# A cached-attention block on one core: start of TensorE's work, order of K's transposes, and where its instruction pages begin

## The chip, the core and the metric

The kernel runs on one core of a Trainium2 chip. A core has engines with queues of their own that meet through semaphores: TensorE (matmuls, shown as PE, its weight loads as PEld), VectorE (DVE), ScalarE (ACT), GpSimd (POOL) and SyncE (SP), which here issues the DMAs. The metric is the device time of the whole kernel in microseconds (us), the median of several runs.

## The reference

```
B, Sq, D = 8, 112, 640;  H, Sk, Dh = 32, 512, 192        # all inputs bf16
q = (x @ wq).reshape(B, Sq, H, Dh).transpose(0, 2, 1, 3)
scores = einsum("bhqd,bhkd->bhqk", q, k_cache) * Dh ** -0.5
o = einsum("bhqk,bhkd->bhqd", softmax(scores), v_cache)
return o.transpose(0, 2, 1, 3).reshape(B, Sq, H * Dh) @ wo
```

A query projection for 896 rows, attention of 112 queries over 512 cached keys for each of 8 x 32 batch and head pairs, and an output projection. K and V are read once each; together they are most of the 117.5 MB that the profile counts as read.

## The kernel before, in words

`build_main` treats the heads in NG = 8 groups of four. A **unit** is one group with one batch entry, so there are NU = 64 units; unit u has g = u // 8 and b = u % 8. All loops are unrolled and every engine's order is written out by hand. (A second, slower kernel stands behind a flag for inputs out of range; it doesn't run here.)

**TensorE per unit i:** `do_S(i)`, scores of unit i, 96 matmuls of 32 rows, four of them abreast; `do_T(i - 2)`, six transposes of the normalised outputs; a slot (i, 0); `do_PV(i - 1)`, 16 matmuls; a slot (i, 1). A slot holds a **pair** or half of one (`do_pair`): a chunk of the query projection of the next group ("Q", 5 steps), or a 128-row tile of the output projection ("O", 6 steps). A step is one weight load and a matmul for each half of the row, into PSUM banks 6 and 7; the second matmul (`held`) uses the weights that are loaded. Before a pair's first step `bank_free` waits until the pair before has been copied out: a Q by ScalarE, an O by VectorE (`do_OE`). FILL cuts the matmuls of chosen slots, all but the first step's, into several narrower ones; this adds instructions and no arithmetic.

**VectorE per unit i:** transposes of K tiles (`do_KT(u, t)`, four a unit, from the landed `kr` to `kt`), the first three of the unit's list; `do_OE` of slot 0; `do_NM(i - 1)`, sums, reciprocals and half of the normalisation; `do_OE` of slot 1; the rest of its transposes. `kt_ahead` says how many tiles are done at the end of unit i: 4(i + 2) and a few more. `kr` has three buffers; SyncE issues K's load of unit u once the transposes of unit u - 3 are done, V's once PV of unit u - 4 is.

**The start:** TensorE keeps itself busy with WARM + 1 matmuls on the identity, transposes four of the seven 128-row tiles of x (`do_X`, one PSUM bank each), which VectorE (m = 0, 2) and ScalarE (m = 1, 3) copy to xT. Then come six chunks of the first group's projection for the first half of the rows (`do_Q0(c, 0)`); their weights are taken from the landed wq by a stride, in four column strips of 32. In the meantime GpSimd reorders the same weights into `wq0` (`reorder`, semaphore gW0). Then the last three tiles of x, S(0), and six chunks for the other half of the rows with `wq0`.

Kernel lines that the text names: L843 x transposes, L847 `held`, L863 and L870 first projections, L905 pairs, L924 S, L945 PV, L956 T, L962 warm-up, L1082 K transposes, L1103 and L1106 copies of O, L1111 copies of x by VectorE, L1180 reorder.

## Time and profile before

| | us |
|---|---|
| median of 12 runs | 401.61 |
| lowest, highest | 399.4, 406.86 |
| the profiled execution, device time | 400.95 |
| its span, first to last instruction | 398.9 |
| TensorE busy | 387.6 |
| VectorE, ScalarE, GpSimd busy | 293.0, 254.2, 140.7 |

"Busy" is the time in which an engine had an instruction in work; TensorE's matmuls overlap, so it is told not from that share but from the distance of their starts whether TensorE goes at its pace. The row of DMA shows 8 to 9 tenths in nearly all of the span, at 350 to 377 GB/s up to 80 us and about 310 after that. "issue" as a releaser means that an engine waited for nothing that the profile shows.

### The profile page before, as it was taken

The page shows a single profiled execution, that of the slowest core. Times are in us where ns is not written, and L with a number is a line of the kernel's source. Part 1 is how long each engine was busy: PE and PEld are TensorE (multiplying, and loading weights), DVE is VectorE, ACT ScalarE, POOL GpSimd, SP SyncE. Part 2 cuts the span into 40 slices and gives each one's busy share as a digit, 9 for nine tenths or more (in the row PEclk, how much of TensorE's full clock was granted, in tenths as well). Part 3 has the DMA queues.
Part 4 walks back from the last instruction along what each step waited for, and adds up shares of the span by engine and source line. Part 5 has one row for each costly group of instructions (what it writes and reads, how often), then busy time and mean ns, then how long its engine had stood idle before and what let it go on. Part 6 is the DMA issues. An engine that isn't in the chain of part 4 may idle for free.

```text
span 398.9 us, 20213 instructions
## 1 busy us (share of the span) xinstructions
PE 387.6 (97%) x9073; PEld 243.1 (61%) x8291; DVE 293.0 (73%) x569; ACT 254.2 (64%) x550; POOL 140.7 (35%) x420
## 2 busy tenths in 40 slices
PE   7999999999999999999999999999999999999995
PEld 3556564656656555565665666656565665667672
DVE  1667768787796686876787776886788677799833
ACT  3667764766656765558756676566774766666662
POOL 6513543243333253333451254232344223223320
PEclk9999999999999999999999999999999999999999
DMA  8999999999998999989999999989999889999711
GB/s 275 377 372 351 350 353 363 356 314 317 348 329 272 318 325 291 302 287 298 339 317 307 302 305 321 335 274 313 296 306 318 263 276 341 314 293 286 228 37 67
DMA packets 88443, 120.04 MB, mean 301 GB/s; under 512 B 9760, under 2 KB 88352, under 8 KB 88352
## 3 DMA queue, kind: packets, MB, share of 16 engines
q1 hardware_dynamic: 88352, 118.72, 90.0%
q8 instruction: 69, 1.13, 1.2%
q14 instruction: 22, 0.18, 0.2%
HBM read 117.54 MB, written 1.15 MB: 298 GB/s over the span
## 4 chain that ended last, share of the span: by engine, by line
PE 86%; SPq 5%; DMA 3%; DVE 3%; issue 2%; DVEq 0%
PE ps L847 20%; PE ps L945 20%; PE ps L924 19%; PE ps L905 18%; PE ps L956 6%; SPq L1290 5%; DMA kr<-in_k_cache_dram 3%; DVE kt L1082 2%; PE ps L870 2%; PE ps L863 1%; DMA xs<-in_x_dram 1%; PE ps L843 1%; DVE xs L1106 0%; DVE acc L1103 0%; DVE acc L1106 0%
## 5 line engine op out<-in xcount | busy, mean ns | idle before, releaser
L1082 DVE STREAM_TRANSPOSE kt<-kr 128x384 int32<-128x384 int32 x256 | 191.9, 867 | 11.2 <-DMA kr<-in_k_cache_dram 10.8
L1023 ACT ACTIVATE pT<-ps 128x448 bf16<-128x448 f32 x256 | 130.7, 562 | 75.9 <-PE ps L924 75.9
L945 PE MATMUL ps<-vs,pT 128*128 128x193 bf16 x512 | 95.2, 247 | 1.1 <-issue 1.0
L924 PEld LDWEIGHTS ps<-qT,kt 32*128 32x128 bf16 x6144 | 77.1, 93 | 30.4 <-issue 24.4
L905 PE MATMUL ps<-wos,oT 128*128 128x320 bf16 x342 | 90.7, 289 | 2.2 <-DVE acc L1103 1.5
L847 PE MATMUL ps<-wos,oT 128*128 128x320 bf16 (+3 forms) x470 | 92.1, 267 | 0.2
L1206 POOL TENSOR_SCALAR bad<-rinv 112x4 f32<-112x4 f32 x64 | 14.6, 228 | 214.7 <-DVE rinv L1091 214.7
L924 PE MATMUL ps<-qT,kt 32*128 32x112 bf16 x6144 | 87.7, 208 | 1.1 <-issue 1.0
L945 PE MATMUL ps<-vm,pT 128*128 128x193 bf16 x512 | 85.0, 247 | 0.5 <-issue 0.5
L847 PE MATMUL ps<-xT,wqs 128*128 128x448 bf16 (+4 forms) x282 | 74.5, 309 | 0.0
L905 PE MATMUL ps<-xT,wqs 128*128 128x448 bf16 (+2 forms) x210 | 72.8, 347 | 0.2 <-DVE acc L1106 0.2
L1030 ACT ACTIVATE os<-ps,rinv 112x192 bf16<-112x192 f32 x128 | 46.8, 417 | 38.5 <-DVE rinv L1091 37.3
L1188 POOL COPY vm<-vs 128x384 int32<-128x384 int32 x128 | 61.2, 508 | 17.0 <-issue 8.7
L905 PEld LDWEIGHTS ps<-wos,oT 128*128 128x128 bf16 x342 | 33.2, 97 | 47.3 <-issue 39.4
L1007 ACT ACTIVATE qT<-ps 128x448 bf16<-128x448 f32 x96 | 48.1, 554 | 17.0 <-PE ps L905 10.8
L945 PEld LDWEIGHTS ps<-vs,pT 128*128 128x128 bf16 x512 | 47.7, 97 | 18.0 <-ACT oT L1040 10.6
L1088 DVE TENSOR_REDUCE sm<-ps 112x4 f32<-112x8 f32 x64 | 10.6, 165 | 53.9 <-PE ps L945 53.9
L1106 DVE TENSOR_TENSOR acc<-ps,acc 128x320 f32<-128x320 f32 x84 | 37.2, 485 | 16.5 <-PE ps L905 16.5
L945 PEld LDWEIGHTS ps<-vm,pT 128*128 128x128 bf16 x512 | 46.6, 97 | 4.5 <-issue 1.8
L1040 ACT ACTIVATE oT<-ps 128x672 bf16<-128x672 bf16 x64 | 46.4, 725 | 1.9 <-PE ps L956 1.9
L905 PEld LDWEIGHTS ps<-xT,wqs 128*128 128x128 bf16 x210 | 20.4, 97 | 35.0 <-issue 30.2
L1094 DVE TENSOR_TENSOR os<-ps,rinv 112x384 bf16<-112x384 f32 x64 | 35.7, 558 | 6.5
(42 smaller groups left out, 174.5 us busy)
## 6 DMA issues: line engine op xcount, KB each, us to landing
kr<-in_k_cache_dram SPq DMA_DIRECT2D x256, 192.0 KB, 4.0
vs<-in_v_cache_dram SPq DMA_DIRECT2D x256, 192.0 KB, 3.9
wos<-in_wo_dram SPq DMA_DIRECT2D x48, 160.0 KB, 4.0
wqr<-in_wq_dram SPq DMA_DIRECT2D x35, 192.0 KB, 5.2
out_dram<-xs SPq DMA_DIRECT2D x7, 160.0 KB, 2.1
wqs<-in_wq_dram SPq DMA_DIRECT2D x5, 192.0 KB, 3.8
xs<-in_x_dram SPq DMA_DIRECT2D x2, 320.0 KB, 3.3
xs<-in_x_dram SPq DMA_DIRECT2D x1, 480.0 KB, 5.4
```

The costliest lines, as they stand in the source:

```text
L847: return pe.add_instruction(mybir.InstMatmult(name=nc.get_next_instruction_name(), engine=mybir.EngineType.PE, ins=[pe.lower_ap_or_imm(rhs ...
L905: mm = (pe.matmul if h == hs[0] and f == 0 else held)(ps[:, 6 + h, cs], w, rhs[h][:, cs], q == 0, q == n - 1 and f == cuts - 1)
L924: mm = pe.matmul(ps[:, a, SQ * t:SQ * (t + 1)], kt[u % NT][p, t, c // 2, :, c % 2], qT[g % 2][p, c, SQ * b:SQ * (b + 1)], start=(c == 0), ...
L945: mm = pe.matmul(pv[:, k, e, o0:o0 + DH + 1], pT[u % 2][:, a, t, :], src[:, a, v0:v0 + DH + 1], start=(t == 0), stop=(t == 3), skip_group_ ...
L1007: act.activation(qT[g % 2][:, c, HQ * h:HQ * (h + 1)], ps[:, 6 + (n % 2 if g == 0 else h), 0:HQ], ACTF.Copy).then_inc(aQ, 1)
L1023: act.activation(pT[u % 2][:, a, :, 0:SQ], ps[:, a, 0:4 * SQ].rearrange("p (t q) -> p t q", t=4), ACTF.Exp, scale=scale).then_inc(aEX, 1)
L1030: ins = act.activation(os_[u % 2][:, DH * (2 + e):DH * (3 + e)], pv_of(u)[0:SQ, 1, e, 1:1 + DH], ACTF.Copy, scale=rinv[:, u % 4, 2 + e:3 + e])
L1040: act.activation(oT[:, :, SQ * b:SQ * (b + 1)].rearrange("p (k c) q -> p k c q", k=2), src.rearrange("p k (c q) -> p k c q", c=3), ACTF.Co ...
L1082: dve.transpose(dst, src).then_inc(vKT, 1)
L1094: dve.tensor_tensor(os_[u % 2][:, 0:2 * DH].rearrange("p (e d) -> p e d", e=2), pv[0:SQ, 0, :, 1:1 + DH], rinv[:, u % 4, 0:2][:, :, None]. ...
L1106: ins = dve.tensor_tensor(ob[:, m, cs] if g == NG - 1 else acc[:, m, cs], src, acc[:, m, cs], op=ALU.add)
L1188: ins = gp.tensor_copy(vm[u % NM][:, :, (DH + 2) * h:(DH + 2) * h + DH].bitcast(I32), vs[u % NV][:, :, 32 + DH * (1 + h):32 + DH * (2 + h) ...
```

## The change

- Warm-up: matmuls of 4 x WN = 120 columns instead of 80. The tuple that brings WN also sets WARM to 20; the older line `WARM = 30` stays below it.
- After the first four tiles of x, BRIDGE = 8 matmuls of 128 columns on the identity.
- Tile m = 3 of x is transposed into two banks (3 and 5); ScalarE copies its first two chunks, VectorE the other three, as third of its copies. The counts that others wait for (vX) go up by one.
- Chunks c >= RAW = 4 of the first half use `wq0`, with 5 matmuls of full width instead of 20 of 32 columns, and wait for gW0.
- FILL: the cuts at units 24, 48 and in the last group go; slots (32, 0) and (32, 1) are cut in 2 and 3.
- `kt_ahead`: one tile ahead up to unit 9, then one more every second unit, five from unit 16 (before: one more every fifth unit, five from unit 20).

TensorE's main program goes from 9073 matmuls and 8291 weight loads to 8865 and 8262. The queues of SyncE and GpSimd keep their instructions and order.

```diff
-    FILL = {(24, 0): 5, (24, 1): 6, (48, 0): 4, (48, 1): 5, **{(i, j): 2 for i in range(56, 64) for j in range(2)}}
+    FILL = {(32, 0): 2, (32, 1): 3}
+    WARM, WN, BRIDGE, RAW = 20, 30, 8, 4
     HINT_AT = {"act": 55, "dve": 60, "pool": 53, "sp": 56}
     WARM = 30
...
-        want = min(4 * (i + 2) + min(5, 1 + i // 5), 4 * NU)
+        want = min(4 * (i + 2) + min(5, 1 + max(0, i - 8) // 2), 4 * NU)
...
-                    mm = pe.transpose(psb[:, m, dc * 128:(dc + 1) * 128], xs[:, m, dc * 128:(dc + 1) * 128], ident[:])
+                    mm = pe.transpose(psb[:, 5 if m == 3 and dc >= 2 else m, dc * 128:(dc + 1) * 128], xs[:, m, dc * 128:(dc + 1) * 128], ident[:])
...
-                    W(pe, vX, 2 if h == 0 else 3)
+                    W(pe, vX, 3 if h == 0 else 4)
...
-                    if h == 1:
-                        if c == 0:
+                    if h == 1 or c >= RAW:
+                        if h == 0 and c == RAW:
                             W(pe, gW0, dc + 1)
-                        mm = pe.matmul(ps[:, 6 + n % 2, 0:HQ], wq0[:, dc, 128 * c:128 * (c + 1)], xT[:, dc, HQ:2 * HQ],
+                        mm = pe.matmul(ps[:, 6 + n % 2, 0:HQ], wq0[:, dc, 128 * c:128 * (c + 1)], xT[:, dc, HQ * h:HQ * (h + 1)],
...
-            warm = ident[:, None, 0:20].broadcast_to([128, 4, 20])
-            pe.matmul(ps[:, 7, 0:80], ident[:], warm, start=True, stop=True)
+            warm = ident[:, None, 0:WN].broadcast_to([128, 4, WN])
+            pe.matmul(ps[:, 7, 0:4 * WN], ident[:], warm, start=True, stop=True)
             for j in range(WARM):
-                held(ps[:, 7, 0:80], ident[:], warm, True, True)
+                held(ps[:, 7, 0:4 * WN], ident[:], warm, True, True)
             for m in range(4):
                 do_X(m)
+            for j in range(BRIDGE):
+                (held if j else pe.matmul)(ps[:, 7, 0:128], ident[:], ident[:], True, True)
...
-            for m in (1, 3):
-                evac_x(m)
+            evac_x(1)
+            evac_x(3, 2)
...
             for m in (0, 2):
                 evac_x(m)
+            evac_x(3, 2)
```

## The prediction

> **What bounds the kernel now.** I read the page's engine rows first, then the row of busy tenths and the chain that ended last.

> ```profile
> PE 387.6 (97%) x9073; PEld 243.1 (61%) x8291; DVE 293.0 (73%) x569; ACT 254.2 (64%) x550; POOL 140.7 (35%) x420
> ...
> q8 instruction: 69, 1.13, 1.2%
> ...
> PE 86%; SPq 5%; DMA 3%; DVE 3%; issue 2%; DVEq 0%
> ```

> TensorE is busy 97% of the span and is 86% of the chain; no other engine passes 73%. So a time is won only where TensorE stands still, or where its own work gets shorter. The timeline of TensorE alone shows how regular it is: S takes 1.29 us in every unit, T 0.31, PV 1.35, a full pair of O 1.63 or 1.73, a full pair of Q 1.89 or 1.99. I looked for every place where a stage is longer than that. There are few. The list of waits names their two kinds:

> ```profile
> DVE kt L1082 <- DMA kr<-in_k_cache_dram: 10.8, 5, 3.8
> ...
> PE ps L905 <- DVE acc L1103: 1.5, 2, 0.8
> PE ps L945 <- issue: 1.5, 2, 1.0
> ...
> PE ps L924 <- issue: 1.0, 2, 0.6
> ```

> **Kind one: VectorE hands O's banks back late.** The timelines of VectorE and TensorE around 50 us:

> ```profile
> 49.01 3.02 DVE L1082 STREAM_TRANSPOSE kt<-kr 128x384 int32<-128x384 int32 x4
> 54.01 0.86 DVE L1082 STREAM_TRANSPOSE kt<-kr 128x384 int32<-128x384 int32 x1 [1.98 <-DMA kr<-in_k_cache_dram]
> 54.72 0.86 DVE L1103 COPY acc<-ps 128x320 f32<-128x320 f32 x2
> ...
> 55.24 0.31 PE L905 MATMUL ps<-wos,oT 128*128 128x320 bf16 x1 [0.74 <-DVE acc L1103]
> ```

> O(0,1) left TensorE at 52.99. VectorE stood from 52.03 to 54.01 before a transpose whose K had not landed, and the copies of O's banks stood behind it, so the next pair began at 55.24 instead of 54.34: 0.90 us, and 0.25 us more before its second half. The same happens at 60.08 (K of unit 9): the pair starts at 61.31 instead of 60.36, 0.95 + 0.25. At 115.33 five transposes in a row (111.18 to 114.86, no DMA wait) do it once more: 0.34 + 0.11. **Sum 2.80 us.**

> **Kind two: "issue", a page of instructions that is late.** I counted TensorE's instructions in program order, a weight load and a matmul one each. Every gap that no semaphore explains stands at number 194 + 256k and at no other place: before 15.37 (S of unit 0, 0.78 us over the usual step), 138.95 (PV, 0.68), 151.09 (PV, 1.13), 363.74 (S, 0.63) and 368.06 (S, 0.23).

> ```profile
> 138.20 0.24 PE L945 MATMUL ps<-vm,pT 128*128 128x193 bf16 x1
> 138.95 0.26 PE L945 MATMUL ps<-vm,pT 128*128 128x193 bf16 x1 [0.50 <-issue]
> ...
> 149.88 0.24 PE L945 MATMUL ps<-vs,pT 128*128 128x193 bf16 x1
> 151.09 0.24 PE L945 MATMUL ps<-vs,pT 128*128 128x193 bf16 x1 [0.97 <-issue]
> ```

> **Sum 3.45 us.** The other 63 borders cost nothing. In the packet records a page's fetch starts 0.1 to 3.5 us after the border before it, takes 0.9 to 2.0, and a stalled TensorE went on 1.2 to 1.6 us after the fetch's end. A unit has 245 to 273 instructions, so the border creeps backward through it. Where it lies in S, pages last 5.7 to 5.8 us in most of the kernel. Where it lies in PV they alternate between 4.94 and 6.57, since the halved Q pairs lie unevenly about PV: both PV stalls ended a page of 4.94. In the last group a page lasts 4.85. Short pages stall; long ones don't.

> [...] The 69 fetches of 1.13 MB agree in size and count (17,425 instructions), and 63 of 68 borders are hidden; five are not. [...] the 31 warm-up matmuls of 80 columns start 0.067 us apart, the first 20 transposes of 128 columns 0.107, the projections after 7.04 us of 448 columns 0.187 to 0.190.

> **The change part by part.**

> 1. *Warm-up, bridge, split eviction, order of the start.* The added tuple sets WARM to 20, but the old line WARM = 30 stands two lines below and wins: 31 matmuls of 120 columns, 0.100 us each at half clock, 3.10 us from 1.52 to 4.62. The first transpose came at 3.88 (x had landed); now 0.74 later. 20 x 0.107 = 2.13, results at 6.97. Then the eviction of m = 3: ScalarE took 0.70 us for 640 columns and 0.54 for 448, so about 0.38 for its 256; VectorE 0.49 for 640, so at most 0.36 for its 384, beside it. First projection at 7.45 instead of 7.04. The bridge (8 x 0.053 to 0.107 = 0.4 to 0.9 us behind transposes that leave TensorE at 6.76) ends by 7.2 to 7.6: in that gap, at most 0.15 beyond. Before, chunk 0 stood 0.14 us at 7.95 for the fifth piece of wq (landed 7.9); that now absorbs some. Net about +0.27 us at the end of chunk 0 (0 if the clock rises before the transposes; +0.5 if the bridge runs long).
>    Chunks 4 and 5 with reordered weights: 5 matmuls at 0.190 for 20 that run four abreast at 0.187 a row: +0.03 us in all. GpSimd ends the reordering at 10.21; chunk 4 starts after 11.2, so the added wait costs nothing; without that cover it would hold these chunks, and the fifteen transposes of the later x tiles and S(0) behind them. SyncE's queue and GpSimd's are the same, instruction for instruction.
>    What it does move is border 1: 60 instructions go, 9 come, so it lies at the 76th matmul of S(0), not the 51st: 25 x 0.0135 = 0.34 us later. Natural time 14.54 + 0.27 + 0.03 + 0.34 = 15.18; the page is there at 15.37 to 15.6, its predecessor being crossed in chunk 2 as before. A stall of about 0.3 for 0.78; S(0) ends at some 15.85 instead of 16.06. **-0.2**; from -0.6 (no stall) to +0.9 (a fetch start at the late end of its spread).

> 2. *K transposed later at first, then faster.* Through unit 9 VectorE runs 1 tile ahead instead of 2, so the first tile of unit i+2 goes behind O's copies. For unit 6: four transposes end at 52.03 as now, O(0,1) is copied at 53.0 to 53.9, needed at 54.34: no stall. K(8) at 54.0 is wanted at 55.3. In unit 7, O(0,2) is copied some 0.2 us late; K(9), 60.1, is wanted at 60.2 to 61. I carried this on through unit 25 with 0.715 us a transpose, 0.86 for O's two copies, 1.03 for a normalisation, and K landing as now. One stall is left: the step to 4 ahead falls on unit 14 and puts five transposes in front of O(1,2): about 0.4 at unit 15, for the 0.45 at unit 16. 2.80 - 0.15 - 0.40: **-2.25**; from -0.8 (K is late at units 16 to 22 too) to -2.7.

> 3. *Page borders.* Before: 17 of them (units 17 to 24 and 40 to 48) from pairs to PV. With FILL at unit 32 alone there is one such zone, borders 26 to 34, then S up to unit 55 and the start of S. Of the some seven short pages of the two old zones two stalled, 1.81 us; the new zone has three or four. In the last group the cuts go, a unit falls from 264 to 254 instructions, so a page, its border in S, grows by some 0.05 us only; two of eight stalled there, 0.86 us. I take 0.9 + 0.7 for the 2.67: **-1.1**; from -2.67 (none) to +2.

> 4. *Fewer pieces.* Pairs at unit 24 take 1.73 and 2.17 instead of 1.63 and 1.99, at 48 1.71 and 2.15: 0.10 + 0.18 + 0.08 + 0.16 = 0.52 goes. At 32, 10 + 16 extra pieces at about 2.5 ns: 0.06 comes. Last group: halves in two pieces 0.925 against 0.91, PV behind them 1.36 against 1.35, over some eight units 0.2. **-0.65**, -0.4 to -0.7.

> Sum: -0.2 - 2.25 - 1.1 - 0.65 = -4.2. The profiled execution took 400.95 (span 398.9 and 2.05 around it), so 396.75. It lies 0.66 under the median of 401.61; most of that I carry over: **397.3**.

> **Rivals.**
> - *Late pages stay as frequent as they were* (0.16). For: two of seven is a small sample[...]. Then part 3 is nothing: 398.5.
> - *K becomes the wait again* (0.14). From unit 16 on K(i+2) is wanted as first transpose, one unit earlier than now. K(18) landed at 109.4, wanted at 108.7; K(22) at 132.3, wanted at 131.5. Against: K's load waits for the transposes of unit u-3, which come earlier as well. If it doesn't move, five evictions of O stall by some 0.4, 2.0 of part 2's 2.25 is lost: 399.4.
> - *Slower: every short page stalls* (0.06). Place: units 25 to 31 and 57 to 63, some ten pages under 5.1 us; price 0.6 to 1.1 each, 8 us against 2.67 now, less 3.1 from the other parts: 403.8 with the 0.66. It decides once fetches start over some 2.6 us after the border before in nearly all of them. Against: only 2 of 8 in the last group did.
> - That the change doesn't do what it says is true of the warm-up count; it costs the 0.74 us named in part 1, mostly covered.

> **How the numbers follow.** The likeliest case (0.64) gives 397.3. Its bounds added, and the first two rivals, give 395.0 to 400.2; the slow rival and the upper part of the second are left out. A measurement can tell about 0.3% (1.2 us) from no change. The likeliest case is faster nearly always, the first rival in 0.95, the second in 0.65: 0.87 faster, 0.08 the same, 0.05 slower.

> **What would show it.** Right: no wait of L906 (now L905) for acc near 54 and 60 us; VectorE's waits for kr behind the copies of O; a remaining 0.4 near 106; warm-up to 4.6 and first projection near 7.45; gaps by "issue" only at 194 + 256k, fewer than five. Wrong: waits for acc or kt at units 16 to 22, issue gaps in most of units 25 to 31 or 57 to 63, or projections at half clock.

## The result, and the profile after

The changed kernel takes **397.34 us** (median of 10 runs, 396.7 to 398.99) beside 402.15 for the kernel before (43 runs, 398.93 to 406.86): a ratio of **0.9891, 95% interval 0.9868 to 0.9913** (4.4 us, 3.5 to 5.3). The ratio is taken from the fast runs alone, so it is not the quotient of the two medians. The forecast was 397.3. The profiled execution took 398.15, with a span of 396.4; that of before 400.95 and 398.9. So the profiles differ by 2.8 us and the medians by 4.8: the profile of before is one of its better runs, that of after one of its worse. What follows keeps the two apart.

The page after: the span, the engine rows, the fetches of instructions, the chain that ended last.

```profile
span 396.4 us, 19973 instructions
...
PE 387.4 (98%) x8865; PEld 243.7 (61%) x8262; DVE 293.2 (74%) x570; ACT 253.9 (64%) x550; POOL 141.4 (36%) x420
...
q8 instruction: 68, 1.11, 1.2%
...
PE 95%; DVE 3%; issue 1%; POOL 0%; DVEq 0%; POOLq 0%
```

TensorE's share of the chain rises from 86% to 95%. The list of waits (engine, line, releaser; us in total, times, longest) has little left of the first kind:

```profile
DVE kt L1085 <- DMA kr<-in_k_cache_dram: 5.6, 2, 3.1
...
PE ps L925 <- issue: 2.5, 3, 1.1
...
PE ps L957 <- DVE os L1097: 0.3, 1, 0.3
```

VectorE stands 5.6 us before K instead of 10.8, and TensorE's row for acc, 1.5 us before, is gone; one weight load still waits 0.3. VectorE's timeline where the first 0.90 us had been lost:

```profile
51.51 3.05 DVE L1085 STREAM_TRANSPOSE kt<-kr 128x384 int32<-128x384 int32 x4
55.56 0.89 DVE L1106 COPY acc<-ps 128x320 f32<-128x320 f32 x2 [1.00 <-PE ps L906]
57.05 0.17 DVE L1091 TENSOR_REDUCE sm<-ps 112x4 f32<-112x8 f32 x1 [0.60 <-PE ps L946]
```

After the four transposes no fifth comes; VectorE waits 1.00 us for TensorE, and no longer the other way round.

The second kind did not thin out as forecast. TensorE's timeline of S in units 2 and 3:

```profile
26.40 1.21 PE L925 MATMUL ps<-qT,kt 32*128 32x112 bf16 x83
28.66 0.33 PE L925 MATMUL ps<-qT,kt 32*128 32x112 bf16 x12 [1.05 <-issue]
...
33.34 1.21 PE L925 MATMUL ps<-qT,kt 32*128 32x112 bf16 x82
35.68 0.37 PE L925 MATMUL ps<-qT,kt 32*128 32x112 bf16 x14 [1.13 <-issue]
```

Two late pages, 1.21 and 1.29 us over the usual step, where before had none. With 0.44 in S(0) this profile has about 2.9 us of late pages; before had 3.45. In PV and in the last group, where before lost 1.81 and 0.86, there is none.

Where the 2.5 us between the spans come from, read from the start of S in each unit (after less before): unit 1 −0.1; unit 6 +2.5 (the pages of S(2), S(3)); unit 8 +0.2 (K's two waits gone, −2.3); unit 21 −0.45; unit 23 −1.6 (no late page in PV); unit 25 −1.9 and unit 49 −2.0 (the cuts at 24 and 48 gone); the end −2.5 (−0.9 for the pages of S(59) and S(60), given back in part by a 0.4 wait at T(58)).

### The profile page after: what moved, and what is told of

Its sections match the earlier page's. It is cut to its first block, busy times and chain, and to the rows that moved or that the text cites. A ratio compares the mean times of both kernels' runs of the same rounds, so it can differ in the third digit from the quotient of the medians.

```text
span 396.4 us, 19973 instructions
## 1 busy us (share of the span) xinstructions
PE 387.4 (98%) x8865; PEld 243.7 (61%) x8262; DVE 293.2 (74%) x570; ACT 253.9 (64%) x550; POOL 141.4 (36%) x420
## 4 chain that ended last, share of the span: by engine, by line
PE 95%; DVE 3%; issue 1%; POOL 0%; DVEq 0%; POOLq 0%
PE ps L848 22%; PE ps L946 21%; PE ps L906 21%; PE ps L925 20%; PE ps L957 6%; PE ps L864 2%; DVE kt L1085 1%; PE ps L871 1%; PE ps L844 1%; DVE acc L1109 0%; DVE xs L1109 0%; DVE os L1097 0%; DVE rinv L1094 0%; POOL ident L1160 0%; PE ps L963 0%
## 5 line engine op out<-in xcount | busy, mean ns | idle before, releaser
L906 PE MATMUL ps<-wos,oT 128*128 128x320 bf16 x342 | 93.0, 298 | 0.8 <-DVE xs L1109 0.7
L848 PE MATMUL ps<-wos,oT 128*128 128x320 bf16 (+1 forms) x340 | 91.3, 296 | 0.1
L848 PE MATMUL ps<-xT,wqs 128*128 128x448 bf16 (+2 forms) x226 | 74.1, 341 | 0.0
L906 PE MATMUL ps<-xT,wqs 128*128 128x448 bf16 (+1 forms) x210 | 73.5, 350 | 0.0
L906 PEld LDWEIGHTS ps<-wos,oT 128*128 128x128 bf16 x342 | 33.2, 97 | 44.2 <-issue 37.0
L1010 ACT ACTIVATE qT<-ps 128x448 bf16<-128x448 f32 x96 | 48.0, 553 | 16.5 <-PE ps L906 11.2
L1109 DVE TENSOR_TENSOR acc<-ps,acc 128x320 f32<-128x320 f32 x84 | 37.0, 481 | 15.6 <-PE ps L906 15.6
L906 PEld LDWEIGHTS ps<-xT,wqs 128*128 128x128 bf16 x210 | 20.4, 97 | 34.2 <-issue 29.4
```

Of the source, the lines that this page charges most:

```text
L848: return pe.add_instruction(mybir.InstMatmult(name=nc.get_next_instruction_name(), engine=mybir.EngineType.PE, ins=[pe.lower_ap_or_imm(rhs ...
L906: mm = (pe.matmul if h == hs[0] and f == 0 else held)(ps[:, 6 + h, cs], w, rhs[h][:, cs], q == 0, q == n - 1 and f == cuts - 1)
L1010: act.activation(qT[g % 2][:, c, HQ * h:HQ * (h + 1)], ps[:, 6 + (n % 2 if g == 0 else h), 0:HQ], ACTF.Copy).then_inc(aQ, 1)
L1109: ins = dve.tensor_tensor(ob[:, m, cs] if g == NG - 1 else acc[:, m, cs], src, acc[:, m, cs], op=ALU.add)
```

## The experiments

Names: K is the new `kt_ahead`, FILL the new places of the cuts, the start all else. b_ kernels are built from before, a_ and c_ from after. Each ratio is to runs of the kernel before on the same chip.

### K alone, and all but K

```diff
 # b_kt: before, with
-        want = min(4 * (i + 2) + min(5, 1 + i // 5), 4 * NU)
+        want = min(4 * (i + 2) + min(5, 1 + max(0, i - 8) // 2), 4 * NU)
 # a_oldkt: after, with the same line turned back
```

> The kernel before with only the new order of K's transposes (kt_ahead). Theory: the waits for acc near 54 and 60 us (2.35 us in the profile before) go because the copies of O no longer stand behind a transpose whose K has not landed; about 0.4 stays near unit 15. Time about 2.2 us under before (ratio 0.9945). Rival: in the changed kernel TensorE was itself 2.6 us late by two late instruction pages in S(2) and S(3), so K was in time there in any case; then this run shows K's lateness again as a wait for kt or acc near units 6 to 9, and the ratio is 0.998 to 1.000.

> The changed kernel with the old kt_ahead. Theory: 2.2 us slower than the changed kernel, 399.5 (ratio to before 0.9935), with waits for acc near 54 and 60 us back. Rival (K was in time only because TensorE was late, or the gain sits elsewhere): 397.3 to 398 (0.988 to 0.990), no such waits.

b_kt: 399.19, ratio 0.9913 (0.988 to 0.9947), 3.5 us. a_oldkt: 399.19, 0.9935 (0.9908 to 0.9962), 0.0044 ± 0.0035 above the changed kernel: 1.8 us. b_kt has the old start and no acc wait at units 6 to 9. Its own late pages make TensorE come to S(6) 1.3 us later than before; but in a_oldkt it comes 2.0 us later, and with the old order the waits are there. So it is the new order that removes them and not a TensorE that comes later; that rival falls. It keeps one wait at unit 15, 1.22 + 0.25. In a_oldkt the acc waits return, but smaller (0.33 + 0.25 and 0.26 + 0.25), since late pages in S(2) and S(3) had already made TensorE 2 us later: a stall upstream pays for part of the next one.

### FILL alone, all but FILL, and its two halves

```diff
 # b_fill: before, and a_oldfill: after turned back
-FILL = {(24, 0): 5, (24, 1): 6, (48, 0): 4, (48, 1): 5, **{(i, j): 2 for i in range(56, 64) for j in range(2)}}
+FILL = {(32, 0): 2, (32, 1): 3}
 # a_2448: after, with
+FILL = {(24, 0): 5, (24, 1): 6, (48, 0): 4, (48, 1): 5}
 # a_lastcuts: after, with
+FILL = {(32, 0): 2, (32, 1): 3, **{(i, j): 2 for i in range(56, 64) for j in range(2)}}
```

> The kernel before with only the new FILL. With the old start the page borders then lie from pairs to T at borders 19 to 27 and again at 51 to 66, that is in the whole last group, where every page lasts 4.9 us. Theory (short pages stall wherever the border lies): some 4 to 6 issue gaps of 0.2 to 1.1 us, the cheaper pairs' 0.65 us is used up, ratio 0.998 to 1.003. Rival (fetches are late by chance alone, the place is nothing): 0.65 us faster, ratio 0.998, no more gaps in the last group than the two of before.

> The changed kernel with the old FILL. With the new start its cuts at units 24 and 48 come just when the border is about to leave S, so hardly any border lies in T or PV (two of 68). Theory: the cuts cost 0.5 to 0.65 us and save nothing, since the changed kernel's nine borders from pair to T did not stall either: 397.9 (ratio 0.9905). Rival (borders in T and PV cost 0.1 us each on the average): 0.3 us faster than the changed kernel.

> The changed kernel with the old FILL's cuts at units 24 and 48 alone, none in the last group. Units of the last group have 245 to 255 instructions as in the changed kernel, but the page borders there lie at the 70th to 86th matmul of S instead of the 1st to 16th. Theory (a late page is seen where TensorE has little work queued ahead of the border[...]): as slow as with the whole old FILL, 400.3 to 401.3, with issue gaps in two to four of the last group's units. Rival (the cuts in the last group are what costs 3.8 us, by more instructions a unit): 397.7 to 398.2, the 0.46 us of its own cuts above the changed kernel.

> The changed kernel with the cuts in the last group put back, 264 instructions a unit as before, page borders there in pairs and PV. Theory of the queued work: hardly any gap, 0.2 us above the changed kernel, 397.3 to 397.9. Rival (more instructions a unit, so shorter pages and late fetches): 400 to 401 with gaps in the last group.

| kernel | median | ratio (95%) | late pages over 0.4 us in its profile |
|---|---|---|---|
| b_fill | 401.06 | 0.9969 (0.9945 to 0.9992) | S0, S2, S10, PV(21) 1.97 |
| a_oldfill | 401.15 | 0.9978 (0.9952 to 1.0004) | S2, S3, S49 |
| a_2448 | 401.53 | 0.9964 (0.994 to 0.9989) | S0, S2, S3, S47, PV(47), S60, S61 |
| a_lastcuts | 399.56 | 0.9909 (0.9878 to 0.994) | S0, S2, S3, PV(58), the end of PV(59), PV(60) |

FILL brought 1.2 us to the kernel before, and turned back within the changed one it costs 0.0087 ± 0.0034, **3.5 us**, where 0.6 was expected. The profile of a_oldfill (398.38, near its lowest) doesn't show them; the median does. In b_fill's last group every page lasts some 5 us and the borders lie from T to PV; if short pages stalled wherever the border lies, most would be late there, and none is by more than 0.2 us. a_2448 has none of the last group's cuts, so its units there are as long as those of after, but the border lies elsewhere; it is as slow as the whole old FILL. TensorE's timeline of its S(61):

```profile
372.31 1.21 PE L925 MATMUL ps<-qT,kt 32*128 32x112 bf16 x83
374.42 0.37 PE L925 MATMUL ps<-qT,kt 32*128 32x112 bf16 x13 [0.90 <-issue]
```

So late pages come there without the last group's cuts, by the place of the border. They are a part of a_2448's loss only: of some 6 us of late pages in this profile 1.5 lie in the last group, and 1.3 in S(47) and PV(47). a_lastcuts puts these borders into PV and the pairs, which I then thought as safe as the start of S. They were late there three times; one of them:

```profile
364.81 0.33 PE L946 MATMUL ps<-vs,pT 128*128 128x193 bf16 x2
365.89 0.33 PE L946 MATMUL ps<-vm,pT 128*128 128x193 bf16 x2 [0.75 <-issue]
```

So PV and the pairs are not safe either. By its runs a_lastcuts can't be told from the changed kernel (0.7 ± 1.5 us slower), and whether its cuts matter beside the place no run parts: b_fill, with borders in the same stages and without these cuts, was late there by 0.2 us at most.

### The start

```diff
 # b_ktfill: before, with K and FILL of after (the old start)
 # a_wn20: after, with
-    WARM, WN, BRIDGE, RAW = 20, 30, 8, 4
+    WARM, WN, BRIDGE, RAW = 20, 20, 8, 4
```

> The changed kernel with the old start (warm-up of 80 columns, no bridge, m = 3 copied whole, six chunks with strided weights). Borders of units 0 to 3 lie at the 51st to 59th matmul of S instead of the 76th to 84th. Theory: the new start buys no time itself (about -0.1 us at S(1)), and its border place costs 1 to 2 us in S(2) and S(3); against that 25 borders instead of 10 lie from T to pair, at 0.05 us each. Time 396.3 to 397.4. Rival (the start is worth what it is for, TensorE busy and at full clock for the first projections): 397.8 to 399, above the changed kernel.

> The changed kernel with warm-up matmuls of 80 columns, the same count of instructions, so the same borders. Theory: transposes start at 3.9 instead of 4.6 us, the first projection near 6.75 instead of 7.46, its chunk 0 then ends with the fifth piece of wq (7.9) at 8.15 instead of 8.4; the page in S(0) is not earlier by more than 0.25, so S(1) starts 0 to 0.3 us earlier: 397.0 to 397.4. Rival (the longer warm-up is what brings the full clock in time): first projections at half clock in this run, up to 1 us slower.

b_ktfill: 397.49, 0.9864 (0.9826 to 0.9903). a_wn20: 397.48, 0.9865 (0.9829 to 0.9901). Neither differs from after beyond its interval: the new start brings nothing that the median shows, and the wider warm-up in particular nothing. (In a_wn20 the full clock came at 7.30 us and the first projection at 7.36, not at 6.75 as expected, since x landed 0.48 us late.) The profiles show that it is not idle, though. The first projections of b_ktfill, on TensorE's timeline:

```profile
7.24 7.71 PE L870 MATMUL ps<-xT,wqs 128*32 128x448 bf16 x120 [0.84 <-DVE xT L1111]
```

The same 120 took 6.02 us before. Until 11.05 us their rows start 0.373 us apart, then 0.189: the full clock came only then, and S(0) began at 15.83 instead of 13.93. Not all of it stays: the page in S(0), late before, is in time here, so S(1) begins 1.1 us later than before; and since its page in S(3) is in time too, b_ktfill is 0.2 us ahead of after from S(4) on. In the other thirteen profiles the full clock came between 4.2 and 7.7. What sets its time no profile shows. The windows view gives TensorE as busy in 2.56 of 3.40 us in b_ktfill's stretch 4.2 to 7.6, in 2.95 of 3.40 ahead of before's full clock at 6.54: the gap of 0.84 between transposes and projections, which the old start leaves, lies in the first stretch whole, in the second with 0.35. That the gap is what delays the clock is my estimate from these two. The bridge fills it, as TensorE's timeline of after shows:

```profile
4.61 2.34 PE L844 MATMUL ps<-ident,xs 128*128 128x128 bf16 x20
6.74 0.31 PE L969 MATMUL ps<-ident 128*128 128x128 bf16 x1
6.85 0.66 PE L848 MATMUL ps<-ident 128*128 128x128 bf16 x7
7.46 0.75 PE L871 MATMUL ps<-xT,wqs 128*32 128x448 bf16 x12
```

The full clock falls into it: up to 7.06 the starts of the bridge's matmuls are 0.107 us apart, from there on 0.056.

A nearer comparison is c_mid, the last kernel below: a warm-up as long as b_ktfill's, but with the bridge, and the full clock at 7.72. The windows view, b_ktfill first, then c_mid (the second number is the length, the third TensorE's busy time; the 1.00 of the clock tells nothing here, since in before and after its record begins only with the full clock, at 6.54 and 7.07):

```profile
4.20:7.60 3.40, 2.56 (x28) 2.13 (x31) 0.98 (x2) 1.41 (x2) 1.53 (x4) 1.00 1.04 342
```

```profile
4.30:7.70 3.40, 3.40 (x35) 2.06 (x29) 1.34 (x3) 1.09 (x2) 1.69 (x4) 1.00 1.03 335
```

That speaks for the bridge, with one profile on each side. How often the clock comes late without it can't be told from four profiles with the old start, of which one shows it.

The new start has a price as well, by the 25 matmuls by which it moves the borders of the first units. In all eight profiles with these borders (after, after_again, c_kt and the five a_ kernels) the pages in S(2) and S(3) are late, at the 84th and the 83rd matmul, S(3) by 0.5 to 1.6 us. In the four with the old start the border in S(3) lies at the 57th and is never late; S(2), at the 59th, is late in three of them.

### Can it be made better?

```diff
 # c_kt: after, with WN = 20 and
-        want = min(4 * (i + 2) + min(5, 1 + max(0, i - 8) // 2), 4 * NU)
+        want = min(4 * (i + 2) + 1 + sum(i >= s for s in (10, 12, 17, 19)), 4 * NU)
 # c_pg: c_kt, with borders at the start of S in units 0 to 8 and the last group
+    WARM, WN, BRIDGE, RAW = 90, 7, 8, 6
+    FILL = {(8, 0): 5, (8, 1): 6, (32, 0): 5, (32, 1): 6}
 # c_mid: c_pg, with borders in the middle of S there
+    WARM, WN, BRIDGE, RAW = 30, 20, 8, 6
+    FILL = {(16, 0): 5, (16, 1): 6, (40, 0): 5, (40, 1): 6}
 # c_pg and c_mid: the wait for gW0 moves back to the other half's first chunk, the line WARM = 30 goes
```

Beside them the changed kernel ran once more.

> The changed kernel once more, as the measure for the three others. Both theories: ratio to before about 0.988 to 0.989; late pages in S(0), S(2) and S(3) of 2 to 3 us in all, none in the last group; 0.4 to 0.5 us at unit 15.

> The changed kernel with K's steps ahead at units 10, 12, 17 and 19 instead of 10, 12, 14 and 16, and warm-up matmuls of 80 columns. Page borders within 2 matmuls of the changed kernel's. Theory: the 0.5 us before the pair of unit 15 goes, since no unit with an O in its second slot, or followed by one in the first slot, gets five transposes; the warm-up is worth nothing. 0.3 to 0.7 us under the changed kernel. Rival (VectorE is late at another unit instead, 16 to 22, as K comes later): no gain, a wait for acc at another place.

> As the kernel with the new steps of K, but with the borders moved: 91 warm-up matmuls of 28 columns (the same warm-up time), all six first chunks with strided weights, and cuts of 5 and 6 at units 8 and 32. Borders of units 0 to 8 lie at the 7th to 25th matmul of S, those of units 57 to 63 at the 1st to 15th, and only four of 68 lie from T to pair. Theory of the queued work: the late pages in S(2) and S(3) are gone or under 0.5 us in all, 1.5 to 2 us less, for 0.5 us of cuts: 395.8 to 396.6 by the scale on which the changed kernel has 397.3. Rival (in units 0 to 4 the fetch is late by so much, DMA at 370 GB/s, that no place hides it): the gaps stay at 2 to 3 us, 0.2 to 0.5 us above the changed kernel.

> As the kernel before this one, with a warm-up of 31 matmuls of 80 columns and the same cuts at units 16 and 40: the same number of cuts and the same work, 60 instructions fewer ahead of S(0), so that borders lie at the 37th to 54th matmul of S in units 0 to 8 and at the 30th to 45th in the last group. Theory of the queued work: late pages in units 0 to 4 (1 to 3 us) and in two to four units of the last group: 2 to 4 us above the kernel before this one. Rival (the place in S is nothing): the same time within 0.5 us.

after_again: 398.54, 0.9894 (0.9854 to 0.9933). Its profile shows K's last weak place, the wait that the prediction put at 0.4 for unit 15. VectorE's timeline, after_again first, then c_kt:

```profile
106.99 2.23 DVE L1085 STREAM_TRANSPOSE kt<-kr 128x384 int32<-128x384 int32 x3 [1.02 <-DMA kr<-in_k_cache_dram]
109.07 0.86 DVE L1109 TENSOR_TENSOR acc<-ps,acc 128x320 f32<-128x320 f32 x2
```

```profile
104.65 2.98 DVE L1085 STREAM_TRANSPOSE kt<-kr 128x384 int32<-128x384 int32 x4
107.47 0.88 DVE L1109 TENSOR_TENSOR acc<-ps,acc 128x320 f32<-128x320 f32 x2
```

Five transposes stand ahead of O's evictions, K lands 1.02 us late for the third, and TensorE waits 1.61 + 0.25 us; c_kt has four there, and no acc wait at all. A K that lands as late would hold the third of four as well; what the new steps take away is the fifth. **c_kt: 397.51, 0.9862 (0.9825 to 0.9899)**, 1.0 us under after_again, in the direction expected; but the intervals overlap, and b_ktfill and a_wn20 (0.9864, 0.9865) are level with it.

c_pg: 400.18, 0.9925 (0.9893 to 0.9957): a miss. In units 0 to 4 only one page was late, by 0.22 us, as the theory of the place says (after, after_again and c_kt lost 1.4 to 2.5 in S(2) and S(3)). Some of it went at once: S(3) now waited 0.7 us for ScalarE, which waited 0.8 us for GpSimd's copy of V. And the pages that hold the larger cuts at units 8 and 32 last only 3.1 to 3.5 us, and the border after next lies late in S of units 9 and 33: 1.91 and 1.03 us late. The first cost more than its own length. TensorE's timeline:

```profile
71.25 0.32 PE L924 MATMUL ps<-qT,kt 32*128 32x112 bf16 x10 [1.75 <-issue]
...
71.95 0.30 PE L847 MATMUL ps<-wos,oT 128*128 128x320 bf16 x1
...
72.79 0.47 PE L905 MATMUL ps<-wos,oT 128*128 128x320 bf16 x1
73.06 0.47 PE L847 MATMUL ps<-wos,oT 128*128 128x320 bf16 x1
```

and by stretches (the third number from the end is the granted clock):

```profile
72.50:75.80 3.30, 3.30 (x18) 1.91 (x13) 0.89 (x2) 1.55 (x4) 0.00 (x0) 0.50 0.99 315
76.00:80.00 4.00, 4.00 (x120) 2.41 (x113) 3.21 (x7) 2.04 (x5) 1.62 (x5) 1.00 0.99 331
```

From 72.44 to 75.86 TensorE ran at half clock, the matmuls of 320 columns 0.27 us apart instead of 0.135; some 1.7 us went that way. With the two pages that is 4.6 us. On the scale of the expectation, where the changed kernel has 397.3, the expected time is missed by about 3 by the median, and by close to 5 by this run (401.76).

c_mid, 400.29, 0.9931 (0.9906 to 0.9956), was to be slower than c_pg by 2 to 4 and equals it, as the rival said (the place is nothing). c_pg's own losses at its cuts spoil this pair, though; it neither supports nor refutes the place.

### All borders counted

In the 14 profiles I took every border of a page after the first and called it late where the step over it is more than 60 ns above the usual step. Of 929 borders 70 are late. At every one of them that is late by over 0.1 us TensorE went on 1.0 to 1.6 us after the end of that page's fetch, so the stall is a wait for the page. S is divided at its 25th matmul.

| units | start of S | rest of S | T, PV, pairs |
|---|---|---|---|
| 0 to 7 | 1 of 8 | **34 of 104** | |
| 8 to 55 | 1 of 191 | 12 of 371 | 5 of 139 |
| 56 to 63 | **0 of 39** | **12 of 40** | 5 of 37 |

In the last row place is mixed with the cuts: all 39 are from kernels without the last group's cuts, and nine of the twelve from before, b_kt and a_oldfill, which have them. Without the cuts (a_2448, c_mid) it is 3 of 16, fewer but still apart from 0 of 39.

Length and place can be parted at S(59) and S(60). Their pages are the shortest of the kernel outside of cuts, 4.1 to 4.3 us, whatever the version. With the border at the start of S, 0 of 12 are late (after, a_oldkt, a_wn20, after_again, c_kt, c_pg); with it further in S, 7 of 10 (before, b_kt, a_oldfill: 6 of 6; a_2448, c_mid: 1 of 4). So the length is not the cause; of the cuts that is not shown.

The fetch records of the last group fit. In after a fetch begins from 0.5 us ahead of the border before it to 2.1 behind, and ends 2.2 to 4.4 us before the page is needed. In a_2448 and a_oldfill it begins 1.0 to 3.6 us behind and ends 1.3 to 2.5 before, at 12 of 14 borders under 2.0: hardly more than the 1.0 to 1.6 us in which a stalled TensorE went on. Why a fetch begins sooner when the border lies at S's start is not shown. What differs is the work just ahead of the border: there a half pair and PV, over 2 us in 41 instructions; within S as many are some 0.3 us (an estimate: 192 instructions in 1.29 us).

## Why the prediction was right, and where not

**1. The start: right in its times, incomplete in its worth.** Warm-up to 4.61 (4.62 forecast), first projection 7.46 (7.45), the page in S(0) 0.44 late for 0.78 (0.3 forecast), S(1) 0.1 us earlier (0.2). The prediction took from before's profile that the clock is full at the first projection (rows 0.187 to 0.190 us apart from 7.04); with that start it can come later, at 11.05 in b_ktfill. And it moved border 1 by 25 matmuls but did not follow the borders after it, of which those in S(2) and S(3) then cost 2.5 us.

**2. K's order: right.** Forecast −2.25; −3.5 ± 1.4 on the kernel before and −1.8 ± 1.4 within the changed one hold it from both sides, and the waits went by the mechanism named. The rest of 0.4 at unit 15 was 0.25 + 0.25 in the first profile, as forecast, but 1.61 + 0.25 in the repetition and 1.22 + 0.25 in b_kt: two things add up. In the repetition TensorE came to that pair 0.9 us earlier than in after, in b_kt 1.2 us, having lost less to late pages; and K, which a_wn20 had by about 105.9 us, came at 106.99 in the repetition and 106.19 in b_kt, where I had taken it "as now". The rival "K becomes the wait again" has this one place and not the five it named.

**3. Page borders: a fair total from a wrong mechanism.** "Short pages stall; long ones don't" is the step that failed. Two late pages in PV and two of eight in the last group looked like a matter of length. The lengths were misread as well: 4.94 and 6.57 us are distances from one PV to the next; from border to border before's pages in those zones take 4.7 to 6.1 us without their stalls. The two that stalled have 5.1, and the shortest, of 4.81 (to 161.53 us) and 4.67 (to 303.05), were in time. At S(59) and S(60) pages of one length are late in 0 of 12 cases with the border at the start of S and in 7 of 10 further in it, and in b_fill pages of some 5 us are in time: the place of the border decides there, not the length, and what the last group's cuts add to it is open. Hence also the term itself: I left 0.7 us of stalls in the last group, and after has none; I left nothing in units 1 to 7, and it has 2.5. One profile against one gave about 0.5 in all, not 1.1. Neither profile is the measure: outside of the first units the same place is late in one profile and in time in another, with a rate that depends on the place (units 8 to 55: 1 of 191 at the start of S, 12 of 371 in the rest), and a single execution shows a draw. In S(2) and S(3) it is no chance: with this start they are late in all eight profiles. By the medians parts 3 and 4, forecast together at −1.75, are −1.2 ± 0.9 on the kernel before and −3.5 ± 1.4 within the changed one. The second lies above the forecast with its whole interval, so the term was undersized there; which value FILL has in general stays open.

**4. Fewer pieces: right where it can be seen.** The cuts at 24 took 0.28 and are gone (forecast 0.28), those at 48 0.24 (0.24), those at 32 cost 0.10 (0.06). That forecast took 2.5 ns for each of 26 pieces, which holds for O (at 24 0.10 us for 40 pieces); those of Q took 4.5 (0.18 for 40). Of the 0.2 forecast for the last group some 0.06 can be seen.

**The sum** −4.2 stands against −4.8 by the medians and −4.4 by the ratio, and against 0.9864 (−5.5, 3.9 to 7.0) for K and FILL without the start. The total was right with errors of both signs under it, and so in part by luck. For the profiled execution 396.75 was forecast; it took 398.15, since S(2) and S(3) took 2.5 that the sum didn't have and the last group gave 0.7 that it had kept. The rival with late pages as frequent as before would have read its support from the profile of after (three for five, nearly as much time) but its time of 398.5 (0.9923) lies outside the measured interval. The range's upper end of 400.2 is not what the parts' upper bounds add up to (+0.9 − 0.8 + 2 − 0.4 = +1.7, so 403.3); nothing else rests on it. The slow rival is refuted: no page of units 57 to 63 is late in after. That the added `WARM = 20` does nothing was as told, and a_wn20 shows that the warm-up's width is of no weight.

**The spread** was not forecast. Runs of before reach over 7.9 us, and those of b_fill, a_oldfill, a_2448, c_pg and c_mid over 5.2 to 8.1; those of after over 2.3, of b_kt, b_ktfill, a_wn20, after_again and c_kt over 1.5 to 2.7, with 6 to 12 runs each. No one trait of the kernels parts the wide from the narrow: b_kt has the old cuts, and c_pg the borders of the last group at the start of S. But the mean granted clock of the runs does. c_pg's profiled run, with its 3.42 us at half clock in 399.7, has 0.996. Of 119 runs of before with a clock on record 25 have 0.996 or less, and in each of three series their median lies 2.4 to 2.9 us above that of the others. In the six series of narrow spread none of 48 runs has a clock under 0.998, in the seven others 15 of 122. So runs with a lower clock for a while are a part of the spread, and the changed kernel showed none; that the clock was halved in them as in c_pg is an estimate from their means.

**Open:** what makes a fetch late in units 0 to 7, where DMA moves 350 to 380 GB/s (a lighter DMA was not tried); why PV's borders of the last group are late in a_lastcuts and not in b_fill; why b_kt's runs lie close together and b_fill's don't; what lowers the clock in before's longest runs, whose traces were not kept.

## What to carry to other kernels

## What the runs showed of the hardware

- A late page can cost more than its stall: after one of 1.91 us c_pg ran for 3.42 us at half clock (granted clock 0.50), and after the PV(21) stall of 1.97 us b_fill did not (1.00 from 150 to 158 us). Of 119 runs of before 25 have a mean clock of 0.996 or less, c_pg's run 0.996.
- The full clock at the start came between 4.2 and 7.7 us in 13 profiles and at 11.05 in one, in kernels that differ little there.
- In the last group borders at the start of S were late in 0 of 39 cases; further in S in 3 of 16 with the same units of about 254 instructions, and in 9 of 24 with cut units of about 264.
